# Moving four small steps by a round in the opening of a threshold-attention and SoLU kernel

## The chip, the cores and the metric

The kernel runs on one core of a Trainium2 chip. The metric is device time in microseconds (us) of one execution. The core has a matrix engine (TensorE, PE in the profile, with PEld for its weight loads), a vector engine (VectorE, DVE), a scalar engine (ScalarE, ACT), GpSimd (POOL) and a queue engine (SyncE, SP). Each engine takes its instructions in the order in which the program issues them, and waits for another engine through semaphores. Matrix products land in PSUM, and the copies in this kernel are nearly all issued by SP.

## The reference

Two blocks in a row. The attention has 8 batches, 8 heads, 576 rows and 64 columns per head. The result is 4608 tokens of 512 columns, and each token then goes through a feed-forward block of 1024 columns.

```python
scores = scale * np.matmul(q, k.transpose(0, 1, 3, 2))
thresh = np.max(scores, axis=-1, keepdims=True) - tau
scores = np.where(scores >= thresh, scores, -1000000000.0)
attn = np.exp(scores - max); attn = attn / (sum + 1e-09); attn @ v
...
h = x @ w_in                     # 4608x512 @ 512x1024
sm = softmax(h); solu = h * sm
ln = (solu - mean) / np.sqrt(var + 1e-06) * g_ln
out = ln @ w_out                 # 1024x512
```

The weights `w_in` and `w_out` arrive as 64-bit floats, so the kernel converts them to 32 bits on the chip; `g_ln` is multiplied into the rows of `w_out`.

## The kernel before, in words

The attention is cut into 144 *slots*, 18 to a batch. A slot is 128 query rows (two heads side by side) against all 576 keys. Two slots make a unit, whose product with v is one job. One turn of the main loop is a *round*, and round r issues the scores of slot r. The order of issue on each engine is the order of the calls in the loop, written by hand; the loop only picks which large PE job goes into a round.

A round r does this. PE makes the scores (`scores`, L434) into two PSUM banks, which exist once, so the scores of round r+1 wait until ACT has read those of round r. DVE takes the row maxima (`maxes`, L455), ACT does the threshold (`ramp`, L470) and two exponentials (`exps`, L479), POOL scales the rows of slot r-1 (`normalise`, L486 to L489), DVE transposes them (`blocks`, L501). After the second slot of a unit SP copies the transposed blocks across partitions to `wT` (L510, L512). Some rounds later PE multiplies by v (`attend_steps`, L542) and ACT copies the result out of PSUM (`attended`, L572). The round at which this is due stands in `pv_due`: the unit's second slot plus 3, plus 1 for the units listed there. It is done at or after that round if a pair of PSUM banks is free and the PE job of the round allows it. There are two such pairs; each half of the feed-forward's first product takes or holds one until DVE has formed h times exp(h) (`ff_mul`, L635).

A token tile of 128 rows goes through these steps in the feed-forward, each at a fixed distance from the round of its second half product (`by`): maximum (`ff_max`, L620) and exponential (`ff_exp`, L629) in the same round, `ff_mul` a round later, statistics (`ff_stats`, L650 to L661) two rounds later. Three rounds later ACT writes the normalised tile `V` (`ff_norm`, L671), DVE normalises `u` in place (`ff_norm2`, L676), and SP swaps quarters between them by four copies (`ff_swap`, L687). Then DVE transposes V to `uT` (`ff_turn`, L697) and PE makes the second product in two halves (`ff_o`, L710). For the first tile these rounds are 11 and 12 (first product), 15 (V, u, swap), 16 (transpose), 17 and 18 (second product).

The weights come in 16 pieces of 128 rows, one a round: pieces 0 to 7 are `w_in`, 8 to 15 are `w_out`. In round x-1 the words of piece x are combined on DVE (`weight_b`, L308); in round x POOL adds the exponent bits (`weight_c`, L332). For a piece of `w_out`, ACT then multiplies by its 128 gains of g_ln (`weight_f`, L340), and after each odd piece SP copies two pieces with the partition halves exchanged (`weight_d`, L347, two copies of 256 KB). The last of these copies, for pieces 14 and 15, is read by the last half of the first tile's second `ff_o`. A variable `w2_done` allows `ff_o` from round 16 on.

From round 14 on some scores rounds first transpose keys and queries of a later head pair on PE into the free part of the score banks (L379), and `keeps` copies them to SBUF: `keep` runs on ACT (L388, L390 under ACT) or DVE.

On SP the order from round 9 on is: loads of w_out pieces, copies of pieces 8 and 9 (round 9), `wT` of slots 8 and 9 and four copies of k for head pairs 4 and 5 (round 10), the last weight load, copies of pieces 10 and 11 (round 11), `wT` of slots 10 and 11 and four copies of q for pairs 4 and 5 (round 12), copies of pieces 12 and 13 (round 13), `wT` of slots 12 and 13 (round 14), swap, copies of pieces 14 and 15, k for pairs 6 and 7 (round 15), `wT` of slots 14 and 15 (round 16), q for pairs 6 and 7 (round 17).

Of the kernel before, what the change touches and what calls it, by code (L numbers as in the profile page):

```python
# [20 lines left out]
def kernel(  # L21
# [206 lines left out]
    def piece(x):  # L228
        if x < 2 * NP:
            c, hf = divmod(x, 2)  # L230
            cols = slice(512 * hf, 512 * hf + 512)
            return w_in[P * c : P * c + P, cols], w1[:, c, cols], W_UNIT
        c = x - 2 * NP
        return w_out[P * c : P * c + P], w2[:, 2 * c], gs[:, c : c + 1]

    NW = 2 * NP + NC

    def in_bits(x):
        return wide and 0 <= x < 16
# [35 lines left out]
    def weight_m(x):  # L275
        if not wide:
            return
        d = raws[x]
        d["m"] = m = work.tile([P, 512], I32, tag="xe", bufs=1, name="em")
        hi = d["hi"]  # L280
        if in_bits(x):
            nc.vector.tensor_scalar(
                out=m.bitcast(F32), in0=hi.bitcast(F32), scalar1=2.0**-112, scalar2=None,
                op0=ALU.mult,
            )
            nc.vector.tensor_scalar(
                out=m, in0=m, scalar1=0x7FFFFFFF, scalar2=3,
                op0=ALU.bitwise_and, op1=ALU.logical_shift_left,
            )
            return  # L290
        nc.vector.tensor_scalar(
            out=m, in0=hi, scalar1=0xFFFFF, scalar2=0x100000,
            op0=ALU.bitwise_and, op1=ALU.bitwise_or,
        )
# [42 lines left out]
    def weight_f(x):  # L337
        if wide and x >= 2 * NP:
            _, dst, unit = piece(x)
            nc.scalar.activation(out=dst, in_=dst, func=AF.Copy, scale=unit)  # L340

    def weight_d(x):
        c = x - 2 * NP
        if c > 0 and c % 2:
            pair_of = w2.rearrange("p (c two) n -> p two c n", two=2)[:, :, c - 1 : c + 1]
            for r in range(2):
                nc.sync.dma_start(out=pair_of[ROWS[r], 1], in_=pair_of[ROWS[1 - r], 0])  # L347
# [9 lines left out]
    def pair(i):  # L357
        if i not in pairs:
            qT = heads.tile([P, S], F32, tag="qT", bufs=6, name="qT")
            pairs[i] = dict(  # L360
                qT=qT,
                kT=heads.tile([P, S], F32, tag="kT", name="kT"),
                qe=heads.tile([P, ST], F32, tag="qe", name="qe"),
            )
        return pairs[i]

    def turn(room, i, nm, ms):
        raw = whole_rows[i, nm]
        for x, m in enumerate(ms):
            for r in range(2):  # L370
                nc.tensor.matmul(  # L371
                    out=room[ROWS[r], 64 * x : 64 * x + 64], lhsT=raw[ROWS[r], m],
                    rhs=ident[ROWS[r], ROWS[r]], start=True, stop=True,
                )
# [9 lines left out]
    def keep(room, i, nm, ms, by_act):  # L384
        of = room[:, 0 : 64 * len(ms)].rearrange("p (m x a) -> p m a x", a=2, x=32)
        to = pair(i)[nm + "T"].rearrange("p (a m x) -> p m a x", a=2, m=NK)[:, ms[0] : ms[-1] + 1]
        if nm == "k":
            (nc.scalar.copy if by_act else nc.vector.tensor_copy)(out=to, in_=of)  # L388
        elif by_act:
            nc.scalar.activation(out=to, in_=of, func=AF.Copy, scale=scl)  # L390
        else:
            nc.vector.tensor_scalar(out=to, in0=of, scalar1=scl, scalar2=None, op0=ALU.mult)
# [18 lines left out]
    def scores(s, items):  # L411
        b, kind, hp, r = slots[s]
        ps = [ps_mm.tile([P, 1024], F32, tag=f"s{h}", name="s_ps") for h in range(2)]

        kept = {}
        x = S
        for i, nm, ms in items:
            for j in range(2):
                room = ps[j][:, x : x + 64 * len(ms)]
                turn_beside(room, i, nm, ms, j)  # L420
                kept.setdefault(j, []).append((room, i + j, nm, ms))
            x += 64 * len(ms)
        for ks in (slice(SM, S), slice(0, SM)):
            for h in range(2):
                for y in range(2):
                    if kind < 2:
                        d = pairs[b * NP + hp]
                        t = 32 * NK * r + P * kind
                        t += 64 * y
                        lhsT = d["qT"][ROWS[h], t : t + 64]  # L430
                    else:
                        d = pairs[b * NP + r + 2 * y]
                        lhsT = d["qe"][ROWS[h]]
                    nc.tensor.matmul(  # L434
                        out=ps[h][ROWS[y], ks], lhsT=lhsT, rhs=d["kT"][ROWS[h], ks],
                        start=True, stop=True,
                    )
        live[s] = dict(ps=ps, kept=kept)

    def keeps(s, r):  # L440
        for room, i, nm, ms in live[s]["kept"].get(r, []):
            keep(room, i, nm, ms, r == 0 or s <= NW)

    def maxes(s, loose):
        d = live[s]
# [29 lines left out]
    def exps(s):  # L475
        d = live[s]
        d["sm"] = sm = small.tile([P, 2], F32, tag="sm", name="sm")
        for x, w in enumerate(d["w"]):
            nc.scalar.activation(  # L479
                out=w, in_=w, func=AF.Exp, bias=ntau, scale=1.0, accum_out=sm[:, x : x + 1]  # L480
            )
# [184 lines left out]
    def ff_norm(t):  # L666
        d = ffn[t]
        rs, nb = d["norm"]
        d["V"] = V = work.tile([P, 2, DFF // 2], F32, tag="V", bufs=1, name="V")
        u = d["u"].rearrange("p (g n) -> p g n", g=2)  # L670
        nc.scalar.activation(out=V, in_=u, func=AF.Identity, bias=nb, scale=rs)  # L671
# [73 lines left out]
    PER = NS // B  # L745
    LAG_PV = 3

    pv_due = []
    for s, (b, kind, hp, r) in enumerate(slots):
        if r == 1:  # L750
            pv_due.append((s + LAG_PV + (s < 6 or s in (11, PER - 1, PER + 9)), (b, kind, hp)))

    def first_slot(i):
        return PER * (i // NP) + 2 * (i % NP)
# [23 lines left out]
    for i in range(2 * NP, NPAIR, 2):  # L778
        b, hf = divmod(i // 2, 2)
# [29 lines left out]
    with tc.manual_schedule():  # L809
# [31 lines left out]
        pieces = {r: x for r, x in enumerate(range(1, NW))}  # L841
# [5 lines left out]
        rnd = 0  # L847
# [6 lines left out]
        begin, middle, late, norms = {}, {}, {}, {}  # L854
        while True:
# [5 lines left out]
                break  # L861
            for job in begin.pop(rnd, []):
                job()
            if rnd in norms:
                ff_norm(norms.pop(rnd))
            if rnd == NS:
                pairs_free += ["s0", "s1"]
# [19 lines left out]
            if more:  # L887
                room = 1
                if busy and quarter > 1 and preps and rnd + 4 < first_slot(preps[0][2]):
                    room = 0  # L890
                if room and preps and preps[0][0] <= rnd:
                    items = preps.pop(0)[1]
                scores(rnd, items)
                if rnd == 0:
                    turn(tiles[1][:, 256:], 0, "q", range(4, NK))
                    keep(tiles[1][:, 256:], 0, "q", range(4, NK), True)
                    pairs_free += tags
                idle = quarter == 0 and cur is None and (
                    prev is None or bool(pv_due) and pv_due[0][0] <= rnd
                )  # L900
                loose = idle and rnd > NW
                if loose:
                    keeps(rnd, 0)
                    keeps(rnd, 1)
                maxes(rnd, loose)
                ramp(rnd, 0)
                if rnd == 0:
                    weight_e(1)
                    weight_m(1)
                if not loose:  # L910
                    keeps(rnd, 0)
                    keeps(rnd, 1)
                ramp(rnd, 1)
                exps(rnd)
            if rnd in whole:
                whole_pair(whole[rnd])
            if rnd - 1 in live:
# [62 lines left out]
            if attending is not None:  # L980
# [3 lines left out]
                b, kind, hp = attending  # L984
# [16 lines left out]
            if rnd in pieces:  # L1001
                x = pieces[rnd]
                ahead = x + 1 < NW and x + 1 not in early
                if ahead and x >= 4:
                    weight_e(x + 1)
                weight_b(x)
                for y in ASK.get(x, ()):
                    weight_load(y)
                if ahead:
                    if x < 4:  # L1010
                        weight_e(x + 1)
                    weight_m(x + 1)
            if rnd - 1 in pieces:
                weight_f(pieces[rnd - 1])
                weight_d(pieces[rnd - 1])
                w2_done = pieces[rnd - 1] == NW - 1
            for job in load_at.pop(rnd, []):
                job()
# [34 lines left out]
```

## Time and profile before

| | |
|---|---|
| three runs | 854.49, 855.9, 856.76 us, median 855.9 |
| profiled execution, first to last instruction | 854.9 us (the listed times include what lies around the span) |
| busy | PE 819.9, DVE 674.6, PEld 620.5, ACT 570.0, POOL 496.1 us |
| PE busy from 200 to 800 us | 597.8 of 600 us |
| PE busy from 0 to 54 us (the first rounds) | 38.4 us |
| PE busy from 69.86 to 76.98 us (round 12's product with v) | 3.83 of 7.12 us by the stage view |
| granted TensorE clock, mean | 0.985 |

Times in the profile are us from the first instruction. A row of the timeline gives start, duration, engine, line, operation, output and inputs, how many were merged, and in brackets how long the engine had been idle and what it was waiting for. "xN" is the number of instructions: a 32-bit product shows as two passes. In the rows of DMA issues the last number is the median time from issue to landing. The stage view gives, for a stretch of time, each engine's busy time, the granted clock, the share of the 16 DMA engines that was busy and the rate.

In the opening, rounds can be told by the score products: round 12 starts on PE at 65.08 us, round 13 at 76.55, round 14 at 81.48, round 15 at 87.17, round 16 at 93.52, round 17 at 99.60, round 18 at 105.69, round 19 at 110.12.

### The profile page before, as it was taken

To read this page: it belongs to the slowest core of one execution; us is meant where nothing else is said; L and a number is where in the kernel's file an instruction comes from. 1 tells how busy PE (TensorE), PEld (TensorE's weight loads), DVE (VectorE), ACT (ScalarE), POOL (GpSimd) and SP (SyncE) were. 2 spreads that over 40 slices of the span, in tenths; PEclk is the share of its full clock that TensorE was granted. 3 is DMA by queue.
4 is the path that set the end of the run, shared out by engine and by line. 5 is a ranking of instruction groups with operands and counts; after the bars stand their busy time and mean duration, and the time that the engine had idled before them with its cause. 6 is when DMAs were issued, how large, how long until landed. Compare 5 with 4: busy or idle time off the path is not lost.

```text
span 854.9 us, 36109 instructions
## 1 busy us (share of the span) xinstructions
PE 819.9 (96%) x15363; PEld 620.5 (73%) x15363; DVE 674.6 (79%) x1225; ACT 570.0 (67%) x1127; POOL 496.1 (58%) x945
## 2 busy tenths in 40 slices
PE   6778899999999999999999999999999999999997
PEld 5555677778677787777688877777777777777655
DVE  5997787989788888888788878888888878787361
ACT  6886876777767666667666666666677777775121
POOL 4885656666566656565566666565666655555120
PEclk8899999999999999999999999999999999999999
DMA  9999778798888888887888778887788887655212
GB/s 343 254 249 213 191 194 233 188 259 204 226 229 202 211 185 218 216 216 190 201 215 218 195 177 209 207 217 207 195 221 226 207 188 175 165 137 140 67 38 63
DMA packets 75314, 168.54 MB, mean 197 GB/s; under 512 B 11146, under 2 KB 32658, under 8 KB 75154
## 3 DMA queue, kind: packets, MB, share of 16 engines
q1 hardware_dynamic: 74866, 165.82, 76.7%
q8 instruction: 120, 1.97, 1.0%
q10 hardware_dynamic: 288, 0.43, 0.2%
q14 instruction: 40, 0.33, 0.1%
HBM read 46.14 MB, written 9.44 MB: 65 GB/s over the span
## 4 chain that ended last, share of the span: by engine, by line
PE 83%; DMA 4%; DVE 4%; ACT 3%; issue 2%; POOL 2%; SPq 1%; DVEq 0%; ACTq 0%; POOLq 0%
PE o_ps L710 27%; PE h_ps L605 22%; PE s_ps L434 15%; PE pv L542 14%; DMA wT<-T 3%; PE h_ps L595 3%; ACT w L470 1%; DVE w L455 1%; ACT w L479 1%; DVE T L501 1%; POOL w L489 1%; POOL sm L487 0%; PE s_ps L379 0%; DVE w L308 0%; PE tp L371 0%
## 5 line engine op out<-in xcount | busy, mean ns | idle before, releaser
L710 PE MATMUL o_ps<-w,uT 64*64 64x256 f32 x4608 | 269.5, 376 | 2.2 <-issue 1.6
L470 ACT ACTIVATE w<-s_ps,nth 128x576 f32<-128x576 f32 x280 | 196.8, 738 | 105.6 <-DVE nth L455 88.6
L455 DVE CUSTOM_DVE_ANT_0 w<-s_ps,tau_t 128x576 f32<-128x576 f32 x280 | 200.0, 751 | 83.5 <-PE s_ps L434 52.4
L710 PEld LDWEIGHTS o_ps<-w,uT 64*64 64x64 f32 x4608 | 221.8, 133 | 55.4 <-ACT xh L572 12.0
L489 POOL TENSOR_SCALAR w<-w,sm 128x576 f32<-128x576 f32 x288 | 220.6, 778 | 14.3
L501 DVE STREAM_TRANSPOSE T<-w 128x576 f32<-128x576 f32 x288 | 207.7, 756 | 22.6 <-POOL w L489 22.3
L605 PE MATMUL h_ps<-w,xh 64*64 64x512 f32 x1856 | 220.8, 589 | 0.0
L479 ACT ACTIVATE w<-w,ntau 128x576 f32<-128x576 f32 x288 | 219.6, 767 | 0.0
L542 PEld LDWEIGHTS pv<-wT,v 64*64 64x64 f32 x5760 | 172.6, 136 | 39.8 <-issue 16.7
L434 PE MATMUL s_ps<-kT,qT 64*64 64x512 f32 (+1 forms) x2048 | 175.8, 416 | 13.4 <-ACT w L470 11.3
L542 PE MATMUL pv<-wT,v 64*64 64x128 f32 (+1 forms) x5760 | 173.9, 263 | 8.3 <-DMA wT<-T 7.4
L605 PEld LDWEIGHTS h_ps<-w,xh 64*64 64x64 f32 x1856 | 118.4, 133 | 77.2 <-issue 43.6
L486 POOL TENSOR_SCALAR sm<-sm 128x2 f32<-128x2 f32 x144 | 34.2, 237 | 186.5 <-ACT w L479 182.8
L487 POOL TENSOR_TENSOR sm<-sm,mone 128x2 f32<-128x2 f32 x144 | 106.7, 741 | 12.0
L434 PEld LDWEIGHTS s_ps<-kT,qT 64*64 64x64 f32 x2048 | 72.7, 137 | 21.7 <-ACT w L470 16.2
L572 ACT COPY xh<-pv 128x256 f32<-128x256 f32 x64 | 25.4, 396 | 80.9 <-PE pv L542 80.9
L671 ACT ACTIVATE V<-u,nb,rs 128x1024 f32<-128x1024 f32 x36 | 44.7, 1240 | 40.5 <-POOL nb L661 33.6
L697 DVE STREAM_TRANSPOSE uT<-V 128x1024 f32<-128x1024 f32 x36 | 44.1, 1225 | 15.9 <-DMA V<-u 15.6
L479 ACT ACTIVATION_READ_ACCUMULATOR w<-w,ntau 128x1 f32 x288 | 55.4, 192 | 0.0
L676 DVE TENSOR_SCALAR u<-u,rs,nb 128x1024 f32<-128x1024 f32 x36 | 34.9, 971 | 19.5 <-ACT V L671 17.9
L635 DVE TENSOR_TENSOR u<-h_ps,u 128x1024 f32<-128x1024 f32 x36 | 42.8, 1190 | 9.4 <-ACT u L629 9.4
L620 DVE TENSOR_REDUCE hm<-h_ps 128x1 f32<-128x1024 f32 x36 | 42.9, 1193 | 4.9 <-PE h_ps L595 2.7
(77 smaller groups left out, 553.5 us busy)
## 6 DMA issues: line engine op xcount, KB each, us to landing
wT<-T SPq DMA_DIRECT2D x160, 288.0 KB, 6.5
wT<-T SPq DMA_DIRECT2D x64, 576.0 KB, 5.5
v<-in_v_dram SPq DMA_DIRECT2D x16, 576.0 KB, 6.0
V<-u SPq DMA_DIRECT2D x144, 64.0 KB, 3.5
out_dram<-ob SPq DMA_DIRECT2D x71, 128.0 KB, 2.6
q<-in_q_dram SPq DMA_DIRECT2D x28, 288.0 KB, 6.1
k<-in_k_dram SPq DMA_DIRECT2D x27, 288.0 KB, 6.4
qT<-flip SPq DMA_DIRECT2D x48, 144.0 KB, 3.2
```

The costliest lines, as they stand in the source:

```text
L434: nc.tensor.matmul(out=ps[h][ROWS[y], ks], lhsT=lhsT, rhs=d["kT"][ROWS[h], ks], start=True, stop=True,)
L455: nc.vector.tensor_tensor_reduce(out=w, in0=ps[:, 0:S], in1=(zero if loose else tau_t).to_broadcast([P, S]), scale=1.0, scalar=BIG, op0=AL ...
L470: nc.scalar.activation(out=d["w"][x], in_=d["w"][x] if d["loose"] else d["ps"][x][:, 0:S], func=AF.Prelu, bias=d["nth"][x], scale=-1.0, al ...
L479: nc.scalar.activation(out=w, in_=w, func=AF.Exp, bias=ntau, scale=1.0, accum_out=sm[:, x : x + 1])
L487: nc.gpsimd.tensor_tensor(out=sm, in0=sm, in1=mone, op=ALU.pow)
L489: nc.gpsimd.tensor_scalar(out=w, in0=w, scalar1=sm[:, x : x + 1], scalar2=1.0, op0=ALU.mult, op1=ALU.mult)
L501: nc.vector.transpose(out=T[:, :, r, h, :], in_=w)
L542: nc.tensor.matmul(out=to, lhsT=d["v"][ROWS[u], (h0 + h - u) % 4, m,], rhs=rhs, start=m == 0, stop=m == NK - 1,)
L605: mm = nc.tensor.matmul(out=h[ROWS[y], f], lhsT=x[ROWS[r], c, ROWS[y]], rhs=w1_parts[ROWS[r], c, part ^ r], start=part == 0 and c == 0, st ...
L671: nc.scalar.activation(out=V, in_=u, func=AF.Identity, bias=nb, scale=rs)
L697: nc.vector.transpose(out=uT, in_=d["V"].rearrange("p y (m x) -> p m y x", x=32))
L710: nc.tensor.matmul(out=d["o"][ROWS[z], 512 * (r ^ other) : 512 * (r ^ other) + 256], lhsT=d["uT"][ROWS[r], m].rearrange("p y x -> p (y x)" ...
```

## The change

Five edits, all in the order of issue; no instruction is added or removed.

- The product with v of slots 8 and 9 becomes due at round 13 instead of 12.
- In round 15 the second of the two `keeps` (a copy of two blocks of k and a scaled copy of five blocks of q) goes from ACT to DVE.
- `ff_norm` in rounds up to 16, which is the first tile's alone, moves from the start of round 15 to behind round 15's two exponentials on ACT.
- `weight_f` of each piece (g_ln) moves one round later, to the end of round x+1.
- `weight_d` moves with it, behind the next round's other SP copies. `w2_done` stays where it was.

```diff
     def keeps(s, r):
         for room, i, nm, ms in live[s]["kept"].get(r, []):
-            keep(room, i, nm, ms, r == 0 or s <= NW)
+            keep(room, i, nm, ms, r == 0 or s <= NW and s != NW - 1)
...
         if r == 1:
-            pv_due.append((s + LAG_PV + (s < 6 or s in (11, PER - 1, PER + 9)), (b, kind, hp)))
+            pv_due.append((s + LAG_PV + (s < 6 or s in (9, 11, PER - 1, PER + 9)), (b, kind, hp)))
...
-            if rnd in norms:
+            if rnd in norms and rnd > NW:
                 ff_norm(norms.pop(rnd))
...
                 exps(rnd)
+            if rnd in norms:
+                ff_norm(norms.pop(rnd))
             if rnd in whole:
...
+            if rnd - 2 in pieces:
+                weight_f(pieces[rnd - 2])
+                weight_d(pieces[rnd - 2])
             if rnd - 1 in pieces:
-                weight_f(pieces[rnd - 1])
-                weight_d(pieces[rnd - 1])
                 w2_done = pieces[rnd - 1] == NW - 1
             for job in load_at.pop(rnd, []):
```

NW is 16 and PER is 18.

## The prediction, made before the changed kernel was run

> **What bounds the kernel now.** I read the page first, then the stage view, then the timelines of PE, SP, ACT and DVE around rounds 12 to 19.
>
> ```profile
> span 854.9 us, 36109 instructions
> ```
>
> ```profile
> 60.00:82.00 22.00, 18.71 (x270) 13.25 (x264) 15.86 (x29) 13.75 (x29) 13.24 (x21) 0.92 1.04 222
> ...
> 91.26:94.68 3.42, 0.93 (x24) 0.55 (x18) 2.31 (x3) 3.42 (x8) 3.32 (x4) 1.00 0.88 229
> 94.68:98.09 3.41, 3.36 (x48) 2.67 (x52) 0.90 (x2) 2.39 (x6) 1.68 (x4) 0.50 0.36 83
> ...
> 125.00:855.00 730.00, 720.53 (x13534) 547.99 (x13526) 574.16 (x1026) 476.10 (x938) 413.64 (x810) 1.00 0.76 190
> ```
>
> The columns are PE, PEld, DVE, ACT and POOL busy, clock, DMA share, GB/s. After 125 us PE is busy 720.5 of 730 us, so a gain or loss in the opening reaches the end undiminished, and I only need the shift at the start of round 19 (110.12). Between 60 and 82 us the DMA engines are full (1.04).
>
> ```profile
> 72.10 0.44 PE L542 MATMUL pv<-wT,v 64*64 64x128 f32 x4 [2.24 <-DMA wT<-T]
> 73.59 3.36 PE L542 MATMUL pv<-wT,v 64*64 64x128 f32 x66 [1.06 <-DMA wT<-T]
> ...
> 78.05 3.80 PE L605 MATMUL h_ps<-w,xh 64*64 64x512 f32 x32
> 81.48 1.45 PE L379 MATMUL s_ps<-ident,k 64*64 64x64 f32 x50
> ...
> 87.17 0.45 PE L379 MATMUL s_ps<-ident,k 64*64 64x64 f32 x11
> ...
> 89.21 2.30 PE L542 MATMUL pv<-wT,v 64*64 64x128 f32 x72
> 93.52 0.68 PE L379 MATMUL s_ps<-ident,q 64*64 64x64 f32 x16 [2.00 <-ACT qT L390]
> ...
> 105.69 1.16 PE L434 MATMUL s_ps<-kT,qT 64*64 64x64 f32 x16
> 106.67 3.63 PE L710 MATMUL o_ps<-w,uT 64*64 64x256 f32 x64
> 110.12 1.45 PE L379 MATMUL s_ps<-ident,k 64*64 64x64 f32 x50
> ```
>
> PE stands still at two places: in round 12 it waits 2.24 and 1.06 us for wT of slots 8 and 9, and in round 16 it waits 2.00 us for ACT's copies of round 15.
>
> **The product with v.** PE was free at 72.10 - 2.24 = 69.86. Without the product in round 12, scores 13 start there. The product does not run in round 13, although it is due: the first half product of tile two takes one pair of PSUM banks, and tile one holds the other until `ff_mul`. So it moves two rounds, behind the half product of round 14. PE alone would then go: scores 13, 0.98 (106.67 - 105.69), half product 3.43 (81.48 - 78.05), round 14 5.69 (87.17 - 81.48), product 2.30. Round 15 could begin at 69.86 + 0.98 + 3.43 + 5.69 + 2.30 = 82.26 instead of 87.17, 4.9 us sooner. That is the most this edit can give.
>
> What is late next are the loads of q for head pair 4, which round 15 transposes.
>
> ```profile
> 78.97 1.24 SPq L142 DMA_DIRECT2D q<-in_q_dram  x2
> ```
>
> ```profile
> q<-in_q_dram SPq DMA_DIRECT2D x2, 144.0 KB, 6.9
> ```
>
> The last two were issued from 78.97 and landed 6.9 us later, at about 86.2. The same bytes are ahead of them after the change (wT of slots 8 to 11, copies of pieces 8 to 11, k, a weight piece; only their order differs), and the DMA engines had no room between 60 and 82. I take 86.2 for the landing. Then follow 20 transposes of the second head (of the kind of which 50 take 1.45: 0.6) and the scores (0.98, with a start of 0.2): round 15's scores end at 88.0. Before, DVE began on them at 89.52 (row below). **Term 1: -1.5 us.** Its ends are -4.9 (loads land as PE needs them) and -0.4 (1.1 us of it lost to half clock).
>
> **Round 15 on ACT and DVE.** I now count from this moment, X: 89.52 before.
>
> ```profile
> 90.40 0.72 ACT L340 ACTIVATE w<-w,gs 128x512 f32<-128x512 f32 x1 [1.90 <-POOL w L332]
> 91.03 1.23 ACT L671 ACTIVATE V<-u,nb,rs 128x1024 f32<-128x1024 f32 x1
> 92.16 0.72 ACT L470 ACTIVATE w<-s_ps,nth 128x576 f32<-128x576 f32 x1
> 92.79 0.25 ACT L388 COPY kT<-s_ps 128x128 f32<-128x128 f32 x1
> ...
> 93.92 0.76 ACT L470 ACTIVATE w<-s_ps,nth 128x576 f32<-128x576 f32 x1
> 94.54 0.80 ACT L479 ACTIVATE w<-w,ntau 128x576 f32<-128x576 f32 x1
> ...
> 96.06 0.40 ACT L572 COPY xh<-pv 128x256 f32<-128x256 f32 x1
> ...
> 98.25 0.74 ACT L470 ACTIVATE w<-s_ps,nth 128x576 f32<-128x576 f32 x1 [1.19 <-DVE nth L455]
> ...
> 103.62 1.36 ACT L470 ACTIVATE w<-s_ps,nth 128x576 f32<-128x576 f32 x2
> ```
>
> ```profile
> 89.52 0.76 DVE L455 CUSTOM_DVE_ANT_0 w<-s_ps,tau_t 128x576 f32<-128x576 f32 x1 [0.80 <-issue]
> ...
> 92.36 1.24 DVE L676 TENSOR_SCALAR u<-u,rs,nb 128x1024 f32<-128x1024 f32 x1 [1.40 <-POOL w L489]
> 93.53 1.42 DVE L501 STREAM_TRANSPOSE T<-w 128x576 f32<-128x576 f32 x2
> 97.45 0.76 DVE L455 CUSTOM_DVE_ANT_0 w<-s_ps,tau_t 128x576 f32<-128x576 f32 x1 [2.51 <-PE s_ps L434]
> ...
> 98.81 1.43 DVE L501 STREAM_TRANSPOSE T<-w 128x576 f32<-128x576 f32 x2
> 100.17 1.20 DVE L697 STREAM_TRANSPOSE uT<-V 128x1024 f32<-128x1024 f32 x1
> ```
>
> ACT before: the first ramp comes only at 92.16, after the gains of piece 14 (1.90 of waiting and 0.63) and V (1.13). After the change both are gone from there, and half of the copies between the ramps too, so the ramps end about 2 us sooner and PE's 2.00 us wait in round 16 goes. But V now waits behind the exponentials; DVE's `ff_norm2` overwrites u, which V reads, so it waits for V; and round 14's transposes and round 16's maxima are queued behind it on DVE. From X to round 16's maxima, after: ramp 0.80 after the maxima begin (98.25 - 97.45), 0.63 to the copies (92.79 - 92.16), one pair of copies 0.56 (half of 93.92 - 92.79), second ramp 0.62 (94.54 - 93.92), exponentials 1.52 (96.06 - 94.54), V and the hop 1.33 (92.36 - 91.03), `ff_norm2` 1.17 (93.53 - 92.36), transposes 1.36 (100.17 - 98.81): 7.99. Before: 97.45 - 89.52 = 7.93. **Term 2: +0.06.** What ACT saves, DVE gives back. The pair of copies moved to DVE costs about 0.6 there, where DVE stands idle until V is done: nothing. If V's cover failed, it would be that 0.6.
>
> **Rounds 16 to 18.** M is the start of round 16's maxima (97.45 before, X + 7.99 after).
>
> ```profile
> 93.63 3.12 SPq L687 DMA_DIRECT2D V<-u  x4
> 97.09 1.36 SPq L347 DMA_DIRECT2D w<-w  x2
> 98.50 2.91 SPq L142 DMA_DIRECT2D k<-in_k_dram  x4
> ...
> 102.17 2.72 SPq L512 DMA_DIRECT2D wT<-T  x2
> ```
>
> ```profile
> V<-u SPq DMA_DIRECT2D x2, 64.0 KB, 2.6
> ```
>
> `ff_norm2` ends at X + 6.70, the four swaps go out over 3.12 (the last about 1.9 in), and land 2.6 later: X + 11.2, M + 3.2. Before, `ff_turn` began at 100.17, M + 2.7. So `ff_max` and `ff_exp` of tile two, behind it, are 0.5 later. Then ACT has the gains of piece 15 (0.63, 91.03 - 90.40) ahead of round 17's ramps, which before ended at 103.62 + 1.36, M + 7.53: now M + 8.66. Scores 18 need them: M + 8.77, where before PE started them at M + 8.24. **Term 3: +0.53.**
>
> Last the copies of pieces 14 and 15. Before they left at 97.09. Now SP issues them behind the swap, the k loads and wT of slots 14 and 15: X + 6.73 + 3.12, then to the end of wT's issues 0.05 + 2.91 + 3.48 (104.89 - 101.41): X + 16.3, and the second copy 0.7 later, X + 17.0 = M + 9.0. The gains of piece 15 are ready before (M + 7.3). Who waits: the last half of the first tile's second `ff_o`, at M + 8.77 + 0.98 + 1.73 (half of 110.12 - 106.67) = M + 11.5.
>
> ```profile
> w<-w SPq DMA_DIRECT2D x2, 256.0 KB, 3.8
> ```
>
> ```profile
> w<-w SPq DMA_DIRECT2D x8, 256.0 KB, 5.9
> ```
>
> ```profile
> w<-w SPq DMA_DIRECT2D x1, 256.0 KB, 8.1
> ```
>
> The 3.8 is these same copies before, with the DMA engines at 0.36 just then; 8.1 is one at 70.75, with them full; 5.9 is the median of all eight. Behind three fresh copies of wT the ring is neither empty nor as full as at 70: I take 5.9, landing at M + 14.9. **Term 4: a wait of 3.4 us,** with ends 1.3 and 5.6.
>
> The Trainium skill, page "DMA: Bandwidth & Descriptors", section "Queues, rings and completion order", says that each DMA engine takes descriptors in ring order and that a completion lands only after that engine's earlier writes. By it the 3.8 could not return here, as the copies would land after wT: with 5.9 the sum is as below, with 3.8 it would be 2.1 us less. The rows agree in kind (8.1 with full engines, 3.8 with idle ones); none shows these copies behind a fresh wT.
>
> The other copies are moved too: pieces 8 and 9 behind wT of slots 8 and 9, pieces 10 and 11 behind the next wT and ahead of q, pieces 12 and 13 behind wT of slots 12 and 13 (which now also wait for the moved product to free their buffer, and are needed only in round 16). All are read from round 18 on: nothing. Gains of pieces 8 to 13 take ACT time of equal length a round later, where PE waits for loads: nothing, else 0.6 each.
>
> **Sum.** -1.5 + 0.06 + 0.53 + 3.4 = +2.5 us on a span of 854.9. The median of the runs, 855.9, is 1.0 above that span, which I leave on top: 858.4.
>
> **The rivals.** *No change.* The copies land as fast as before (3.8), term 4 is 1.3: +0.4, 856.3. The transfer rate for it is there: PE's stage at 94.68 to 98.09 used 0.36 of the DMA. Against it: they now follow 1.2 MB of wT. It decides below a landing of 5.9 us.
>
> *Faster.* The loads of q follow their earlier issue and not the bytes ahead: term 1 is -4.9, and with copies that land in 3.8 the sum is -4.9 + 0.06 + 0.53 + 1.3 = -3.0, 852.9. For it: q is issued up to 3 us sooner. Against it: the 1.04. It decides where q lands before 83.3.
>
> *Half clock.* The stretch 91.26 to 94.68 has PE busy 0.93 of 3.42, and the next one is granted 0.50: 3.4 us at half rate cost at most 1.7 us of work. New waits in rounds 14 to 17 may trigger that again; most falls where PE waits anyway (q, copies), so it is none in the sum and +1.7 at most: 860.1.
>
> **How the numbers follow.** A measurement of this kernel tells about 0.3% (2.6 us) from no change. The likeliest is a new wait for the copies, with what half clock adds: slower, 0.47. My sum lies at that edge, its upper ends (8.1, half clock) beyond it. No measurable change: 0.37. Faster: 0.16. The range goes from the faster rival, 853.0, to -0.4 + 0.06 + 0.53 + 5.6 = +5.8, rounded up to 862.0.
>
> **What would show it.** Right: no PE wait in round 12, the product with v after the half product of round 14; PE idle before round 15's transposes of q, with q landing near 86; DVE idle in round 15 until V; PE idle in the middle of `ff_o` in round 18, ended by the DMA of w2. Wrong: round 15's scores done before 86 us, `ff_o` of round 18 running through, or `ff_norm2` not the last before round 16's maxima.

## The result and the profile after

The changed kernel took 860.53 us (median of 13 runs, 857.07 to 865.84), the kernel before 856.6 us beside it. The ratio is 1.0045, with a 95% interval of 1.0026 to 1.0064: the change makes the kernel 3.9 us slower, 2.2 to 5.5 by the interval. Medians are over all runs of a kernel, while ratios and intervals leave out disturbed runs, so the two can differ a little.

The profiled execution is the quickest of the 13 of the changed kernel: its span is 855.2 us, only 0.3 above that of the kernel before. So spans alone do not show the loss; the waits and the stages do.

```profile
span 855.2 us, 36124 instructions
```

TensorE's waits from 54 to 118 us, in the kernel before (in total, times, longest):

```profile
PE pv L542 <- DMA wT<-T: 6.1, 4, 2.2
PE s_ps L379 <- ACT qT L390: 2.0, 1, 2.0
```

and in the changed kernel:

```profile
PE pv L542 <- DMA wT<-T: 2.7, 2, 2.2
PE o_ps L710 <- DMA w<-w: 2.3, 1, 2.3
PE pv L542 <- ACT xh L572: 1.3, 1, 1.3
...
PE s_ps L379 <- ACT qT L390: 0.2, 1, 0.2
```

Of the two waits that the change was put at, round 12's is gone, and of the 2.00 us before round 16's transposes 0.2 is left. In their place PE waits 2.3 us for the copies of w2. Round 10's wait for wT, part of the 6.1 us, stays. In the kernel before its rows were

```profile
57.71 0.44 PE L542 MATMUL pv<-wT,v 64*64 64x128 f32 x4 [2.10 <-DMA wT<-T]
58.87 2.07 PE L542 MATMUL pv<-wT,v 64*64 64x128 f32 x66 [0.72 <-DMA wT<-T]
```

The PE timeline of the changed kernel has the same rows and the new places:

```profile
57.75 0.69 PE L542 MATMUL pv<-wT,v 64*64 64x128 f32 x4 [2.20 <-DMA wT<-T]
58.92 3.89 PE L542 MATMUL pv<-wT,v 64*64 64x128 f32 x66 [0.48 <-DMA wT<-T]
...
83.67 2.19 PE L542 MATMUL pv<-wT,v 64*64 64x128 f32 x70
...
105.75 2.32 PE L710 MATMUL o_ps<-w,uT 64*64 64x256 f32 x36
110.37 1.73 PE L710 MATMUL o_ps<-w,uT 64*64 64x256 f32 x26 [2.30 <-DMA w<-w]
```

The moved product starts at 83.67, behind round 14's half product. The second half of the first tile's `ff_o` is broken in two. And round 10's product (58.92), which no edit touches, took 3.89 us here at half clock, against 2.07 before; it will matter below.

The chain of waits of the changed kernel, from round 15's exponentials on, names each step of the new path:

```profile
90.94 1.52 ACT w L479 x4
92.45 1.14 ACT V L671
...
93.62 0.82 DVE u L676
...
96.38 2.46 DMA V<-u
...
100.03 1.20 DVE hm L620
...
101.25 0.69 ACT u L629
...
103.71 0.50 SPq L347
...
104.26 6.07 DMA w<-w
...
110.37 1.57 PE o_ps L710 x25
```

V stands behind the exponentials, then come `ff_norm2`, the swap, the transpose, `ff_max` and `ff_exp` of tile two, the gains of piece 15 and their copies, the second of which lands 6.07 us after it left.

### The profile page after: what moved, and what is told of

The parts are those of the page before. It is cut to its first block, busy times and chain, and to the rows that moved or that the text cites. A ratio compares the mean times of both kernels' runs of the same rounds, so it can differ in the third digit from the quotient of the medians.

```text
span 855.2 us, 36124 instructions
## 1 busy us (share of the span) xinstructions
PE 818.7 (96%) x15363; PEld 624.5 (73%) x15363; DVE 674.4 (79%) x1227; ACT 571.6 (67%) x1125; POOL 496.7 (58%) x945
## 4 chain that ended last, share of the span: by engine, by line
PE 83%; DMA 6%; ACT 3%; DVE 3%; issue 2%; SPq 1%; POOL 1%; DVEq 0%; ACTq 0%
PE o_ps L710 27%; PE h_ps L605 23%; PE s_ps L434 15%; PE pv L542 14%; PE h_ps L595 3%; DMA wT<-T 3%; ACT w L470 1%; DVE w L455 1%; ACT w L479 1%; DVE T L501 1%; SPq L687 1%; DMA w<-w 1%; DMA raw<-in_moe_w_out_dram 1%; DMA V<-u 1%; DMA kT<-flip 0%
## 5 line engine op out<-in xcount | busy, mean ns | idle before, releaser
L710 PEld LDWEIGHTS o_ps<-w,uT 64*64 64x64 f32 x4608 | 230.5, 133 | 49.0 <-ACT xh L572 11.8
L455 DVE CUSTOM_DVE_ANT_0 w<-s_ps,tau_t 128x576 f32<-128x576 f32 x280 | 200.1, 751 | 77.2 <-PE s_ps L434 44.7
L434 PE MATMUL s_ps<-kT,qT 64*64 64x64 f32 (+1 forms) x2048 | 173.2, 411 | 16.5 <-ACT w L470 13.6
L605 PEld LDWEIGHTS h_ps<-w,xh 64*64 64x64 f32 x1856 | 116.0, 133 | 81.7 <-issue 54.9
L629 ACT ACTIVATE u<-h_ps,hm 128x1024 f32<-128x1024 f32 x36 | 40.3, 1120 | 10.7 <-DMA V<-u 5.4
```

What stands on the lines that cost most here:

```text
L434: nc.tensor.matmul(out=ps[h][ROWS[y], ks], lhsT=lhsT, rhs=d["kT"][ROWS[h], ks], start=True, stop=True,)
L455: nc.vector.tensor_tensor_reduce(out=w, in0=ps[:, 0:S], in1=(zero if loose else tau_t).to_broadcast([P, S]), scale=1.0, scalar=BIG, op0=AL ...
L605: mm = nc.tensor.matmul(out=h[ROWS[y], f], lhsT=x[ROWS[r], c, ROWS[y]], rhs=w1_parts[ROWS[r], c, part ^ r], start=part == 0 and c == 0, st ...
L710: nc.tensor.matmul(out=d["o"][ROWS[z], 512 * (r ^ other) : 512 * (r ^ other) + 256], lhsT=d["uT"][ROWS[r], m].rearrange("p y x -> p (y x)" ...
```

## The experiments

Single executions differ by several us for reasons outside the change, so each kernel is read in two ways: by its ratio over many runs, and by the time that its profile spends in each stretch of the opening. The stretches are worked out from the DVE timeline: the start of the first row maximum (L455) of one round minus that of another. Round 15 to 16 in the kernel before is 97.45 - 89.52 = 7.93 from the rows in the prediction. (The tables use unrounded starts.)

```
rounds             10-15  15-16  16-18  18-19   10-19
before             32.97   7.94   9.43   6.67   57.00
before_again       31.42   8.23   9.43   6.67   55.76
after              32.47   7.73  10.26   8.96   59.42
after_again        31.56   7.72   9.81  11.12   60.21
copies_back        30.77   8.22   9.39   6.66   55.04
last_pair_back     30.87   7.72   9.40   6.67   54.66
v_back             30.90   4.53  11.03  11.03   57.49
copies_only        29.61   4.98  13.56   7.66   55.81
v_only             31.23   8.62  10.57   6.66   57.08
product_only       30.56   5.95   9.43   6.67   52.60
best_no_product    30.29   4.53   9.93   6.66   51.41
best_guess         30.58   4.57   9.90   6.67   51.71
best_again         30.63   5.56   9.43   6.68   52.29
```

Theory: the late copies of pieces 14 and 15 cost the time. Rivals: V behind the exponentials costs it, or chance of the clock.

### The two kernels once more

No edit; the changed kernel and the kernel before were run again.

> The changed kernel once more, for a second profile, since in its first one rounds 10 and 11 ran 3.8 us late at half clock by chance and a 1.6 us gap of the kernel before at 129 us was missing. Theory (the late copies of pieces 14 and 15 are what costs): 3 to 4.5 us slower than the kernel before, and in the profile again a wait of 2 to 4 us for the copies of w2 in the middle of round 18's second product. Rival (it is the clock or chance): the wait is under 1 us in this profile, and the time differs from the first measurement by over 2 us.

Measured: ratio 1.0032 (1.0004 to 1.0059), that is 2.7 us, a little under the 3 to 4.5 expected; median 861.02 against 857.54. In its profile the wait is there again:

```profile
PE o_ps L710 <- DMA w<-w: 2.9, 1, 2.9
```

and what followed the wait ran at half clock (26 passes in 2.49 us, against 1.73 in the first profile):

```profile
111.12 2.49 PE L710 MATMUL o_ps<-w,uT 64*64 64x256 f32 x26 [2.88 <-DMA w<-w]
```

The loss repeats, and so does the wait; the rival of chance falls.

> The kernel before, unchanged, for a second profile and to see what the comparison gives for no change. All five other profiles lose 2.0 to 2.9 us more than the first profile of the kernel before between the maxima of rounds 10 and 11, at half clock, though nothing they change has been issued by then. If that is chance of the clock window: this profile can show it too, and a wait in front of the second product of round 22 of 0 to 3 us. If the changed order did it: rounds 10 to 11 take 5.4 us again. Ratio 1.000 within 0.003 in either case.

Measured: ratio 0.9992 (0.9960 to 1.0025), no difference. Its product in round 10:

```profile
60.77 0.44 PE L542 MATMUL pv<-wT,v 64*64 64x128 f32 x4 [3.41 <-DMA wT<-T]
61.90 3.56 PE L542 MATMUL pv<-wT,v 64*64 64x128 f32 x66 [0.70 <-DMA wT<-T]
```

So the slow round 10 is chance and no effect of the edits. But these are all its waits for wT before 118 us: round 12 does not wait at all. The stretch from round 10 to 15 takes 31.42, even less than in the first profile, which had a quick round 10 and a wait in round 12.

### The copies of w2

Edit of `copies_back`, against the changed kernel:

```diff
-            if rnd - 2 in pieces:
-                weight_f(pieces[rnd - 2])
-                weight_d(pieces[rnd - 2])
             if rnd - 1 in pieces:
+                weight_f(pieces[rnd - 1])
+                weight_d(pieces[rnd - 1])
```

> The changed kernel with the gains and copies of all w2 pieces where they were before; product with v, V and keeps as changed. Theory (the copies cost): the wait in round 18 (2.3 us in the first profile) is gone, the time is 2 to 3 us below the changed kernel, about 857.5 to 858.5 if the kernel before has 856.6. Rival (V behind the exponentials is what costs): within 1 us of the changed kernel, about 860.

Measured: ratio 1.0000 (0.9975 to 1.0024), median 857.59, 3.4 below the changed kernel on the same chip. Round 18's second product runs through:

```profile
104.16 3.63 PE L710 MATMUL o_ps<-w,uT 64*64 64x256 f32 x64
```

The edit that matters is the weights' one. Which of its copies? In `last_pair_back` only piece 15's gains and the copies of 14 and 15 return to round 15 (the gains of piece 14, a round later, stand just ahead of them, so nothing is left out):

```diff
-            if rnd - 2 in pieces:
+            if rnd - 2 in pieces and pieces[rnd - 2] < NW - 1:
                 weight_f(pieces[rnd - 2])
                 weight_d(pieces[rnd - 2])
+            if rnd - 1 in pieces and pieces[rnd - 1] == NW - 1:
+                weight_f(pieces[rnd - 1])
+                weight_d(pieces[rnd - 1])
```

> The changed kernel with only the last pair of w2 pieces treated as before: gains of piece 15 and the copies of pieces 14 and 15 in round 15, the gains of piece 14 and all earlier pieces a round later as changed. Here the output is not the reference's if the copies run ahead of the gains of piece 14; the times are what counts. Theory (the wait for the last two copies alone costs): no wait in round 18 and the same time as with all copies back, 857 to 858, about 3 us under the changed kernel. Rival (the earlier copies, moved behind wT and ahead of the loads, cost by crowding the queue): 859.5 or more.

Measured: ratio 0.9981 (0.9957 to 1.0005), median 856.28 against 857.36; rounds 18 to 19 take 6.67. With this pair and its gains back the loss is gone; the earlier copies moved behind wT cost nothing that shows. (The time lies lower than the 857 expected, inside the spread.) The gains of piece 15 and the copies were not moved back one without the other. In the changed kernel these gains end at 103.07, just when SP comes to the copies (103.09), so there both hold them; in `v_back`, below, the gains end at 100.60 and SP comes to the copies only at 101.82, so there the queue alone does.

### V behind the exponentials

`v_back` is the changed kernel with V at the start of round 15:

```diff
-            if rnd in norms and rnd > NW:
+            if rnd in norms:
                 ff_norm(norms.pop(rnd))
...
-            if rnd in norms:
-                ff_norm(norms.pop(rnd))
```

> The changed kernel with V of the first tile back at the start of round 15; all else as changed. Theory (the copies cost): the wait for the w2 copies in round 18 stays, 2 us or more, and round 16's maxima begin 1.5 to 2 us sooner after those of round 15, so the time falls by at most 2 us, to about 858.5 to 860. Rival (V costs): the time falls to that of the kernel before or under it, 856.6 or less, and the wait in round 18 is under 1 us.

Measured: ratio 1.0018 (0.9992 to 1.0043), median 858.55, between the changed kernel and the one before. Rounds 15 to 16 take 4.53 instead of 7.73, so V's place costs 3.2 us there, more than the 1.5 to 2 expected. DVE has no gap any more between the copies and `ff_norm2`:

```profile
89.06 0.54 DVE L392 TENSOR_SCALAR qT<-s_ps,scl 128x320 f32<-128x320 f32 x1
89.52 1.21 DVE L676 TENSOR_SCALAR u<-u,rs,nb 128x1024 f32<-128x1024 f32 x1
```

But PE still waits for the copies, and then runs at half clock:

```profile
107.93 2.93 PE L710 MATMUL o_ps<-w,uT 64*64 64x256 f32 x26 [2.76 <-DMA w<-w]
```

In this profile rounds 16 to 19 take 22.1, where they take 19.2 and 20.9 in the two of the changed kernel, so 1.1 to 2.8 of the 3.2 is given back. The intervals of `v_back` and of `after_again` overlap widely, so the times alone do not tell the two apart. `v_only` has V's edit alone in the kernel before (the same lines as above, the other way round).

> The kernel before with only V of the first tile behind round 15's exponentials. Theory (V there holds DVE): from round 15's maxima to those of round 16 it takes about 2 us more than before, 10 us instead of 8, with DVE idle until V; no wait for the w2 copies in round 18, since they leave in round 15. Time 1 to 2 us over the kernel before. Rival (V is off the path): 8 us again and no difference.

Measured: ratio 1.0018 (0.9991 to 1.0046), median 860.08 against 856.11. Rounds 15 to 16 take 8.62, 0.4 to 0.7 more than before, not 2: before, V stood in front of the ramps and cost time there too. DVE does wait as expected:

```profile
93.93 1.27 DVE L676 TENSOR_SCALAR u<-u,rs,nb 128x1024 f32<-128x1024 f32 x1 [4.63 <-ACT V L671]
```

There is a second row in it, which bears on the prediction's first term, round 15's transposes waiting for the loads of q:

```profile
85.70 1.03 PE L379 MATMUL s_ps<-ident,q 64*64 64x64 f32 x32 [0.53 <-DMA q<-in_q_dram]
```

The interval takes in no change, so the size of V's cost alone stays open.

`copies_only` has the weights' edit alone, in the kernel before.

> The kernel before with only the gains and copies a round later. Theory: the wait of 2 us or more in the middle of round 18's second product appears here too, and ACT is rid of the 1.9 us wait for piece 14 before round 15's first ramp; net 1 to 3 us slower than the kernel before. Rival (the copies cost only together with the late V): within 1 us of the kernel before, wait under 1 us.

Measured: ratio 1.0001 (0.9978 to 1.0024): no difference, so here the rival was right in time. Rounds 15 to 16 fall to 4.98, since ACT no longer waits for the gains of piece 14 and V is early, and the wait in round 18 is short:

```profile
110.16 1.73 PE L710 MATMUL o_ps<-w,uT 64*64 64x256 f32 x26 [1.00 <-DMA w<-w]
```

In this profile rounds 16 to 18 took 13.56, with a 2.3 us wait for wT in round 16, so it does not show cleanly how much of the gain the late copies take. By the intervals the weights' edit alone is below the whole change (at most 1.0024 against at least 1.0026); that it takes the late V too to make the full loss fits this, and is read from the stretches, not shown by the times.

### The moved product

`product_only` has only this line changed in the kernel before:

```diff
-            pv_due.append((s + LAG_PV + (s < 6 or s in (11, PER - 1, PER + 9)), (b, kind, hp)))
+            pv_due.append((s + LAG_PV + (s < 6 or s in (9, 11, PER - 1, PER + 9)), (b, kind, hp)))
```

> The kernel before with the later product with v alone. By the sum of the prediction the loads of q hold round 15, so of the 4.9 us at most 1.5 are left: 855.1 if the kernel before has 856.6. Rival (q does not hold it, as the first profile suggests, where PE did not wait before round 15's transposes of q): 3 to 4.9 us faster, about 852 to 853.5.

Measured: ratio 0.9994 (0.9966 to 1.0022). Rounds 10 to 15 take 30.56. That is less than in the two profiles of the kernel before, but `copies_only`, `v_only` and `best_no_product`, which keep the product in round 12, take 29.61, 31.23 and 30.29, and all eight with the moved product 30.56 to 32.47. So the move gains nothing in these rounds that the profiles can tell; the reason stands under term 1 below. Rounds 15 to 16 take 5.95 here, against 7.94 and 8.23 before, and round 19 comes 3.2 to 4.4 us sooner after round 10. The ratio shows none of that; this profile stands still for 2.74 us in round 22 (last section).

### A better order

`best_guess` keeps V and the copies where they were, and takes the moved product, the `keeps` on DVE, and only the gains of piece 14 a round later, away from the front of round 15's ramps (the lines of the other two edits are left out here):

```diff
+            if rnd - 2 in pieces and pieces[rnd - 2] == NW - 2:
+                weight_f(pieces[rnd - 2])
             if rnd - 1 in pieces:
-                weight_f(pieces[rnd - 1])
+                if pieces[rnd - 1] != NW - 2:
+                    weight_f(pieces[rnd - 1])
                 weight_d(pieces[rnd - 1])
```

> The kernel before with the later product with v, the second keeps of round 15 on DVE, and only the gains of piece 14 a round later, just ahead of those of piece 15; V and the copies where they were. From the profiles: the maxima of round 16 follow those of round 15 by 4.5 to 5 us (7.9 before, 7.7 changed), no wait for copies, the tile's second product held by the transpose of V as with V back. Time 0 to 3 us under the kernel before, that is 854.5 to 857.5; if what is won is given back in waits for instructions later, no difference.

> The best guess once more, to narrow its interval. If its gain is real: ratio to the kernel before again 0.996 to 0.999. If it was chance: 0.999 to 1.002.

Measured: 0.9973 (0.9947 to 0.9999), median 854.95 against 857.36, and again 0.9972 (0.9944 to 1.0001), 855.17 against 856.11. By the ratios it is about 2.4 us faster than the kernel before; each interval reaches just about to no change, and the two agree. V is done before `ff_norm2` needs it, so DVE goes straight through round 15:

```profile
88.72 0.54 DVE L392 TENSOR_SCALAR qT<-s_ps,scl 128x320 f32<-128x320 f32 x1
89.18 1.27 DVE L676 TENSOR_SCALAR u<-u,rs,nb 128x1024 f32<-128x1024 f32 x1
```

`best_no_product` is this without the line of `product_only`.

> The best guess with the product with v of slots 8 and 9 due at round 12 again. If the move gives nothing because loads pace rounds 10 to 15: those rounds take 31 to 33 us together as in the kernel before, and the time is within 1 us of the best guess, about 855 if the kernel before has 857. Rival (the move is what makes the best guess fast): 1.5 to 3 us slower than the best guess, that is the time of the kernel before.

Measured: 0.9978 (0.9951 to 1.0006), median 854.67: the same as the best guess. So what the best guess gains it has without the product's move. That leaves the gains of piece 14 and the `keeps`, in round 15; neither was tried alone, and the interval takes in no change.

The table tells more than the ratios. From round 15 to 19 (its middle three columns added) the kernel before takes 24.0 and 24.3. With the gains of piece 14 and the `keeps` moved, and V and the last copies at their old places, it is 21.1 to 21.7 (the last three rows). With V late, and those copies and gains back, it is 24.3 and 23.8 (`copies_back`, `last_pair_back`); with late copies and V early 26.6 and 26.2 (`v_back`, `copies_only`); with both late 27.0 and 28.7. These groups differ in the other edits too, so the sums are a reading and no proof: the change held some 3 us of gain in rounds 15 to 19, its late V alone takes about 3 of it back, and its late copies alone about 5.

## Why the prediction was right or wrong

The direction was right: 858.4 forecast, 860.5 measured; +2.5 us against +3.9 (in the second comparison 2.7 by the ratio, 3.5 by the medians). The time lies inside the range, whose top was 862.0. By its own terms, from the stretches, as means of two profiles each:

**Term 1, the moved product, -1.5 us.** Measured from round 10 to 15: 32.0 after, 32.2 before, -0.2. That is the term that was mis-sized, and three steps of it failed.

The loads of q did not hold round 15. The prediction took 86.2 as their landing "after the change" too. In the changed kernel the last two, issued from 80.02, land 4.0 later, the last at about 84.7,

```profile
q<-in_q_dram SPq DMA_DIRECT2D x2, 144.0 KB, 4.0
```

and PE transposes q at 85.9 without a wait. Only `v_only` shows a wait for q there, the 0.53 us above.

Round 12's wait was taken as standing in every execution, from one profile (and PE's "two places" left out the 2.10 and 0.72 us in round 10). Of the 13 profiles only that one has it: its rounds 12 to 13, from maxima to maxima, take 11.99, and its rounds 10 to 11 only 5.44. In all others rounds 10 to 11 take 6.9 to 9.4 (slower landing of wT, half clock), round 12 does not wait, and rounds 12 to 13 take 7.05 to 7.07, with the product there or without it.

What sets these 7.06 us is DVE, which the prediction's "PE alone" left out. In the changed kernel the scores of round 13 begin on PE at 72.29 and take about 1.3, but DVE has `ff_max` to do first, which waits for round 12's half product, and then weights, and goes without a pause into the maxima:

```profile
72.72 1.23 DVE L620 TENSOR_REDUCE hm<-h_ps 128x1 f32<-128x1024 f32 x1 [0.48 <-PE h_ps L605]
73.86 0.68 DVE L308 SCALAR_TENSOR_TENSOR w<-raw,em 128x512 int32<-128x512 int32 x1
...
76.25 0.74 DVE L455 CUSTOM_DVE_ANT_0 w<-s_ps,tau_t 128x576 f32<-128x576 f32 x1
```

In `before_again`, with the product in round 12, the same two DVE steps begin at 74.61 and 78.14, again 3.53 apart. PE, rid of the product, comes to the scores sooner than DVE can read them. Two rounds later the product stands in front of round 15's scores instead: rounds 14 to 15 take 6.3 to 6.9 in the eight profiles with the move, and 5.3 to 5.8 in four of the five without (6.7 in `v_only`, which waits for q). X itself came at 87.97 against the 88.0 foretold, but after 3.7 us of extra delay between the maxima of rounds 10 and 11 (9.18 against 5.44) that no term holds: the number was right by accident.

**Term 2, round 15, +0.06.** Measured -0.4 (7.73 and 7.72 against 7.94 and 8.23). The mechanism was right step by step: ramps sooner, DVE idle 3.5 us until V, maxima directly behind.

```profile
93.62 0.81 DVE L676 TENSOR_SCALAR u<-u,rs,nb 128x1024 f32<-128x1024 f32 x1 [3.54 <-ACT V L671]
```

`v_back` puts the price of V's place here at 3.2 us.

**Term 3, the chain to round 18, +0.53.** Measured in rounds 16 to 18: +0.8 and +0.4. In the first profile half clock has a part in it, from 98.71 to 102.12.

**Term 4, the wait for the copies, 3.4.** Measured in rounds 18 to 19: +2.3 and +4.4, the mean 3.4. The copies were foretold to land at M + 14.9; M is 95.70 in the changed profile and PE resumes at 110.37, M + 14.7. But PE stands only from 108.07, M + 12.4 and not M + 11.5 (36 passes in 2.32 us ran ahead of the wait, where half the job in 1.73 was taken), so the wait itself is 2.3 and 2.9 where 3.4 was foretold; that the mean comes out at 3.4 is luck, made up by the half clock behind the second. The issue had to pass the swap, k and wT first:

```profile
94.47 2.50 SPq L687 DMA_DIRECT2D V<-u  x4
97.01 2.58 SPq L142 DMA_DIRECT2D k<-in_k_dram  x4
99.70 0.62 SPq L510 DMA_DIRECT2D wT<-T  x1
100.36 2.60 SPq L512 DMA_DIRECT2D wT<-T  x2
103.09 2.84 SPq L347 DMA_DIRECT2D w<-w  x2
```

The first of the two landed 6.3 us after its issue (the row has a landing for it alone), the second 6.1 by the chain above, where 5.9 was taken:

```profile
w<-w SPq DMA_DIRECT2D x2, 256.0 KB, 6.3
```

The rule from the Trainium skill, page "DMA: Bandwidth & Descriptors", section "Queues, rings and completion order", spoke for a landing behind wT, and the trace agrees: 6.3 here, and 3.8 again in `best_guess`, where the copies leave ahead of k and wT.

The prediction put the 3.8 down to DMA engines at 0.36. That share is of 94.68 to 98.09, mostly before the copies left. Over the time that they were under way, 97.09 to 101.58, the stage view gives 0.76. Over the second copy's way it gives 0.88 in `best_guess` (94.53 to 98.31) and 0.87 in the changed kernel (104.26 to 110.33): at the same share the one copy took 3.8 and the other 6.1. So how busy the engines were does not tell these landings apart; what stood ahead of the copies in the queue does.

**The sum.** By the stretches the changed kernel is 3.4 us later at round 19 (59.8 against 56.4), and the ratio says 3.9. So nothing of note is missing; the forecast was 0.9 to 1.4 short. Term 1 alone came out 1.3 above its size, and term 2 0.4 below.

**That the opening's shift reaches the end undiminished.** For this loss it holds within the spread. For the gains it does not: `product_only` is 3.8 ahead at round 19 in its one profile and its ratio shows no gain, the best guess is 4.4 ahead in two and keeps 2.4. The last section has the one place found where some of it goes.

**The rivals.** "No change" needed the copies to land in 3.8, "faster" needed q before 83.3 and the copies in 3.8; neither came. Half clock did come, as a part of term 4: behind the wait in `after_again` and `v_back`, for which the sum had nothing.

## What to carry to other kernels

When a step is moved in a queue, follow its transfer to the one who reads it: the copies had been harmless at one place, and one round later they stood behind three other groups of copies and came out in front of the product that reads them. A step that others wait for through an engine in order (V, which DVE's next three jobs stood behind) should leave the critical engine only if those can go ahead of it. And a wait seen in one profile may stand in for another that the next execution has in its place; look at the time between two fixed points before and after it. Where a wait goes from one engine, ask which engine reads its result next, and whether that one was free: here DVE was not.

## What the runs showed of the hardware

Two things had not been expected. The first is how much single executions differ after the opening. From the maxima of round 19 to those of the last round, where all the kernels issue the same work, 13 profiles took 666 to 675 us. A part is one place: 12 of the 13 show PE idle in the middle of round 22's first `ff_o`, with nothing in the profile that it waits for, for 0.6 to 3.7 us. The longest, in `best_again`, and that of the kernel before:

```profile
129.92 5.81 PE L710 MATMUL o_ps<-w,uT 64*64 64x256 f32 x50 [3.72 <-issue]
```

```profile
131.15 3.03 PE L710 MATMUL o_ps<-w,uT 64*64 64x256 f32 x51 [1.59 <-issue]
```

In both profiles one 16 KB transfer of the instruction queue runs in this stretch. The packet times of all the traces say more: in each of the 12, PE goes on 1.3 to 1.6 us after the same transfer of that queue has ended, whether the gap is 0.6 us (ended 129.18, on at 130.74 in `v_back`) or 3.7 (128.63 and 129.92 in `best_again`). In the changed kernel's first profile, which has no gap, PE passes the place at 130.99, 1.6 after the transfer's end at 129.43. So PE very likely waits for instructions that come late; no run moved the transfer to test it. The four profiles that reach round 22 first (123.4 to 125.5 us) have 1.3 to 3.7 us there, the other nine 0 to 2.1, which may be why the best guess, 4.4 us ahead at round 19, ends only 2.4 ahead. This stays open.

The second is the clock. A stretch in which PE was partly busy (0.93 of 3.42 us in the prediction's rows) was enough to halve the next 3.4 us, so the wait for the copies can cost more than its own length: rounds 18 to 19 lost 2.3 us with a wait of 2.30, but 4.4 with one of 2.88. The length is not all; it matters how the wait lies to the stretches of 3.4 us for which the clock is granted. In `after_again` PE was busy 0.82 of 3.42 us up to 111.94, and the next stretch was granted 0.50. In the first profile the wait lies across the border of two stretches, with PE busy 2.54 and 1.99, and the clock stays at 1.00. Where the limit lies the profiles do not show: 1.84 busy was followed by half clock once (`last_pair_back`, up to 94.03), 1.53 was not once (`copies_back`, up to 96.75).
